# When the queries and keys of two pairs of heads are scaled: behind their roots, or in front of their turns

## The chip, the core and the metric

The kernel runs on one core of a Trainium2 chip. The metric is the device time of one execution in microseconds (us). The engines have a queue each and run it in order: TensorE (PE, matrix products; PEld is its weight load), VectorE (DVE), ScalarE (ACT), GpSimd (POOL) and SyncE (SP), which here only issues transfers. An instruction that waits for another engine holds everything behind it on its own queue.

## The reference

There are 8 batch elements of 12 heads, 448 positions and 64 channels a head. The first half is attention with normalised queries and keys, the second an MLP mixer over positions and then over channels. Cut to what matters:

```python
q_n = q / sqrt(mean(q*q, -1) + 1e-6) * g_q          # the same for k
attn = softmax(q_n @ k_n.T / 8)                      # per head, 448 x 448
x = (attn @ v) laid out as (8, 448, 768)
h = relu(x^T @ w_tok1) @ w_tok2                      # over positions: 448 -> 256 -> 448
u = x + h^T
out = u + relu(u @ w_ch1) @ w_ch2                    # over channels: 768 -> 1536 -> 768
```

The weights of the mixer come in 64-bit floats and are converted to 32 bits by the kernel.

## The kernel before

**Work.** The heads go in pairs, 6 pairs to an element, 48 in all, and two pairs at a time (`t`) make an attention step of four parts (`s` = 0 to 3, written `g = 4t + s`). The attention of an element runs beside the mixer of the element before it: two lists of items with a cost each are merged in proportion (`merge`), and the merged list is written out in that order. The engines' queues follow it as written; only the order on SP's queue is chosen by the scheduler. `behind` holds what follows a part's score and value products (`tiled`) in the attention list, `turns` the transposes of the next two pairs.

**Normalising a pair `n`.** Its queries and keys are loaded to `qk_t` (L1371). ACT squares them (`square`, L1391), DVE sums the squares by row (`reduce`, L1408). For two pairs together `roots` forms the reciprocal roots: DVE makes a first guess (`guess`, L1430), then POOL refines it in three rounds of four small instructions (`newton`, L1438 to L1441). `scale` (L420, DVE) multiplies the pair's queries and keys by the roots in place. `turn_qk` then transposes them: for the first two elements ("plain" pairs, `n` under 12) by 16 PE transposes a two pairs (L432), four for each half of a pair, whose results ACT copies out (L438, L440).

**Around the change.** The pairs that it touches are 8 to 11, the last four of the second element. While they are prepared, the attention of pairs 6 to 9 runs beside the mixer of the first element:
- `score` (L458, PE) and its exponentials (L462, ACT); `group_sums` (L499, DVE) adds up exponentials for the softmax's denominators; `values` (L531, PE); the denominators' sums (L511, PE) and their reciprocals (L555 to L577, DVE).
- `tok2` (L879, PE) makes six products of two matmuls, each into one of two PSUM tiles `m_ps`; the addition L884 (DVE) adds a product to `uT` and frees its tile.
- `first_stage` (L969, PE) is the first element's channel mixer.
- `weight_items` converts a chunk of weights: transfers L222, five DVE instructions (L379 for the chunk three items earlier, then L345, L346, L348, L350), one on ACT (L356) and the store L234 or L237.
- POOL forms sums of weights (`some`, L249 to L266).

Of the kernel before, what the change touches and what calls it, by code (L numbers as in the profile page):

```python
# [83 lines left out]
def whole(ctx, tc, shifted, pre, q, k, v, g_q, g_k, moe_w_tok1, moe_w_tok2, moe_w_ch1, moe_w_ch2, out):  # L84
# [67 lines left out]
    st = dict(pre.st)  # L152
# [263 lines left out]
    def scale(p):  # L416

        x, d = pre.by_rows(p, st["qk", p])
        r = st.pop(("rs", p))
        nc.vector.tensor_tensor(out=x, in0=x, in1=r.unsqueeze(2).to_broadcast(list(x.shape)), op=ALU.mult)  # L420

    def turn_qk(p, i):

        qk = st["qk", p]
        if ("qkT", p) not in st:
            st["qkT", p] = pre.qkT[p] if p < len(pre.qkT) else qkT_pool.tile([P, 2, S], F32, name="qkT")[:]
        to = st["qkT", p][:, i, :]
        if pre.plain(p):
            ps = s_tile("t_ps")
            for c in range(NS):  # L430
                o = (i * NS + c) * P
                nc.tensor.transpose(ps[:, c * R:(c + 1) * R], qk[0:R, o:o + P], ident[0:R, 0:R])  # L432
            src = ps[:, 0:S]
        else:
            nc.vector.transpose(out=to, in_=qk[:, i * S:(i + 1) * S])
            src = to
        if i == 0:
            nc.scalar.mul(to, src, g_t[:, 0:1])  # L438
        elif pre.plain(p):
            nc.scalar.copy(out=to, in_=src)  # L440
        if i == 0:
            st.pop(("qk", p))
# [213 lines left out]
    def att_step(g):  # L656


        t, s = divmod(g, 4)
# [50 lines left out]
        n = p + 2  # L710
        ahead, behind, turns = [], [], []
        f = lambda fn, *pairs: [lambda i=i: fn(i, st) for i in pairs]
        scales = lambda n: [lambda i=i: scale(i) for i in (n, n + 1)]
        if g in (1, 5):
            ahead, behind = f(pre.square, g // 4 * 2 + 4), f(pre.reduce, g // 4 * 2 + 4)
        elif g in (2, 6):
            ahead, behind = f(pre.square, g // 4 * 2 + 5), f(pre.reduce, g // 4 * 2 + 5)
        elif g in (3, 7):
            behind = pre.roots(g // 4 * 2 + 4, st)
        elif g in (4, 8):  # L720
            behind = scales(g // 4 * 2 + 2)
        if live and n < NP:
            late = n < 2 * NPAIR + 2
            if t >= NPAIR // 2 and late:
                if s == 1:
                    ahead, behind = f(pre.square, n), f(pre.reduce, n) + f(pre.square, n + 1)
                elif s == 2:
                    behind = f(pre.reduce, n + 1) + pre.roots(n, st) + scales(n)
            elif t >= NPAIR // 2:
                a, b = f(pre.square, n) + f(pre.reduce, n), f(pre.square, n + 1) + f(pre.reduce, n + 1)  # L730
                behind = (a, b + pre.roots(n, st), scales(n), [])[s]
            now = {2: [] if pre.plain(n) else [n], 3: [n, n + 1] if pre.plain(n) else [n + 1]}.get(s, [])
            turns = [lambda q=q, i=i: turn_qk(q, i) for q in now for i in (1, 0)]
# [481 lines left out]

    mixing = set()
    att_items = lambda lo, hi: [it for g in range(lo, hi) for it in att_step(g)]

    run(merge(
        att_items(0, 8) + merge(att_items(8, AHEAD * per + 1), x_items(0, 0)), weight_items(0, BEFORE)))  # L1220
    left, (some, sums) = [], sum_items()
    for b in range(B):
# [24 lines left out]
        if b + AHEAD < B and (shifted or b < 2):  # L1247
            att = att_items(lo, lo + 10) + x_items(b + AHEAD, 0)
            if shifted:
                att += att_items(lo + 10, lo + per)  # L1250
            elif not b:
                step = att_step(lo + per - 1)
                att += att_items(lo + 10, lo + per - 1) + step[:5] + x_items(1, 1) + step[5:]
            else:
                run(att[:6])
                ahead, block, beside, between = big_step(BIG, False)
                att = att[6:] + att_items(lo + 10, lo + per - 1) + ahead + [block] + beside + between
        elif b + AHEAD < B:
            t = (b + AHEAD) * NPAIR // 2
            blocks = [big_step(t + i // 2, i % 2) for i in range(1, NPAIR + 1)]  # L1260
            blocks[4][3].extend(x_items(b + 1, 0))
            early = place(early, blocks, [near(early, at) for at in BLOCKS])
# [263 lines left out]
```

## Time and profile before

| | us |
|---|---|
| median of three runs | 1302.79 (1302.38 to 1304.1) |
| the profiled execution | 1300.44 |
| its span, first to last instruction | 1298.5 |
| PE busy | 1250.2 (96%) |
| DVE busy | 793.8 (61%) |
| ACT busy | 392.3 (30%) |
| POOL busy | 383.4 (30%) |
| L420 on `qk_t`, 112x1024: one instruction | 1.22 |

The page gives busy times of the engines, the chain of work that ended last, and groups of instructions by source line; the timeline gives single instructions in order, with the idle time of the engine before each and the engine that ended it. PE's rows count two for each 32-bit matmul, so a product of L879 is four rows, and four transposes are four rows. Times within the span count from its first instruction.

### The profile page before, as it was taken

To read this page: it belongs to the slowest core of one execution; us is meant where nothing else is said; L and a number is where in the kernel's file an instruction comes from. 1 tells how busy PE (TensorE), PEld (TensorE's weight loads), DVE (VectorE), ACT (ScalarE), POOL (GpSimd) and SP (SyncE) were. 2 spreads that over 40 slices of the span, in tenths; PEclk is the share of its full clock that TensorE was granted. 3 is DMA by queue.
4 is the path that set the end of the run, shared out by engine and by line. 5 is a ranking of instruction groups with operands and counts; after the bars stand their busy time and mean duration, and the time that the engine had idled before them with its cause. 6 is when DMAs were issued, how large, how long until landed. Compare 5 with 4: busy or idle time off the path is not lost.

```text
span 1298.5 us, 20006 instructions
## 1 busy us (share of the span) xinstructions
PE 1250.2 (96%) x7228; PEld 889.8 (69%) x7228; DVE 793.8 (61%) x1229; ACT 392.3 (30%) x781; POOL 383.4 (30%) x641
## 2 busy tenths in 40 slices
PE   5998999997899999999999999999999999999996
PEld 3444444455654577895787868785887868797996
DVE  6988769754655256765658366765558456554233
ACT  5663433222322043312343034311343033300210
POOL 1303440047887012231132222231122322131231
PEclk9999999998999999999999999999999999999998
DMA  9667585997899567685766867595866964386553
GB/s 207 174 183 180 155 226 146 216 258 208 248 275 217 121 148 172 152 229 117 173 167 144 218 141 175 140 224 116 188 156 149 232 140 136 117 200 156 180 174 79
DMA packets 492864, 228.37 MB, mean 176 GB/s; under 512 B 375508, under 2 KB 453332, under 8 KB 492756
## 3 DMA queue, kind: packets, MB, share of 16 engines
q1 hardware_dynamic: 476178, 213.10, 66.6%
q0 software_dynamic: 3584, 12.06, 3.0%
q10 hardware_dynamic: 12994, 1.84, 0.8%
q8 instruction: 59, 0.97, 0.3%
q14 instruction: 49, 0.40, 0.1%
HBM read 184.26 MB, written 42.66 MB: 175 GB/s over the span
## 4 chain that ended last, share of the span: by engine, by line
PE 84%; DVE 6%; DMA 3%; POOL 2%; issue 2%; ACT 1%; SPq 1%; ACTq 0%; DVEq 0%; POOLq 0%
PE m_ps L999 23%; PE m_ps L1065 21%; PE s_ps L458 9%; PE o_ps L531 9%; PE m_ps L879 5%; PE m_ps L969 5%; PE m_ps L1048 4%; PE t_ps L837 2%; PE m_ps L837 2%; DMA ws<-raw 1%; PE m_ps L511 1%; PE d_ps L511 1%; POOL raw L320 1%; PE t_ps L432 1%; DVE raw L348 1%
## 5 line engine op out<-in xcount | busy, mean ns | idle before, releaser
L1065 PE MATMUL m_ps<-hb,unit 128*128 128x224 f32 x1440 | 277.2, 354 | 0.0
L1065 PEld LDWEIGHTS m_ps<-hb,unit 128*128 128x128 f32 x1440 | 271.0, 190 | 8.8 <-issue 7.7
L999 PE MATMUL m_ps<-tu,unit 128*128 128x224 f32 x1008 | 201.6, 355 | 1.3 <-ACT r L1009 1.3
L999 PEld LDWEIGHTS m_ps<-tu,unit 128*128 128x128 f32 x1008 | 189.1, 190 | 15.0 <-issue 9.9
L462 ACT ACTIVATE e<-s_ps 128x448 f32<-128x448 f32 x294 | 138.3, 549 | 174.6 <-PE s_ps L458 166.2
L999 PE MATMUL m_ps<-uT,unit 128*128 128x224 f32 x756 | 153.6, 358 | 13.7 <-DVE hb L1005 11.5
L999 PEld LDWEIGHTS m_ps<-uT,unit 128*128 128x128 f32 x756 | 144.0, 192 | 21.6 <-DVE hb L1005 13.0
L458 PE MATMUL s_ps<-qkT 64*64 64x448 f32 x1260 | 144.6, 545 | 0.8 <-ACT x L819 0.8
L531 PE MATMUL o_ps<-e,v 64*64 64x448 f32 x1148 | 131.4, 538 | 0.3 <-ACT uT L568 0.2
L1005 DVE TENSOR_TENSOR hb<-m_ps,r 128x448 f32<-128x448 f32 x63 | 39.1, 621 | 120.5 <-POOL r L1005 68.9
L499 DVE TENSOR_TENSOR es<-es,e 128x896 f32<-128x896 f32 x90 | 103.2, 1146 | 14.4 <-ACT e L462 9.0
L1005 POOL TENSOR_TENSOR hb<-r,r 128x448 f32<-128x448 f32 x21 | 23.8, 1135 | 245.4 <-ACT r L1021 245.4
L458 PEld LDWEIGHTS s_ps<-qkT 64*64 64x64 f32 x1260 | 45.7, 132 | 69.6 <-issue 60.1
L531 PEld LDWEIGHTS o_ps<-e,v 64*64 64x64 f32 x1148 | 46.4, 133 | 63.1 <-issue 58.4
L1006 ACT ACTIVATE hb<-hb 128x448 f32<-128x448 f32 x84 | 48.4, 577 | 111.8 <-DVE hb L1005 76.6
L879 PE MATMUL m_ps<-w_sb,h 128*128 128x448 f32 x192 | 75.3, 544 | 3.3 <-DVE uT L884 3.3
L1438 POOL TENSOR_TENSOR nt<-rs 128x56 f32<-128x56 f32 (+1 forms) x57 | 19.5, 341 | 198.1 <-DVE rs L1430 195.1
L1080 POOL TENSOR_TENSOR uT<-uT,r 128x448 f32<-128x448 f32 x42 | 51.4, 1240 | 78.3 <-DVE r L1080 46.6
L320 POOL TENSOR_TENSOR raw<-raw 128x128 f32<-128x128 f32 x128 | 68.0, 551 | 16.1 <-DMA ws<-raw 5.9
L884 DVE TENSOR_TENSOR uT<-uT,m_ps 128x448 f32<-128x448 f32 x48 | 29.3, 613 | 63.0 <-PE m_ps L879 63.0
L1005 DVE TENSOR_TENSOR r<-m_ps,r 128x448 f32<-128x448 f32 x42 | 26.1, 622 | 64.7 <-PE m_ps L999 64.7
L1408 DVE TENSOR_REDUCE ms<-sq 128x28 f32<-128x896 f32 (+2 forms) x44 | 47.4, 1080 | 28.6 <-ACT sq L1394 25.0
(141 smaller groups left out, 1585.0 us busy)
## 6 DMA issues: line engine op xcount, KB each, us to landing
unit<-ws SPq DMA_DIRECT2D x267, 384.0 KB, 4.1
raw<-in_moe_w_ch_dram SPq DMA_DIRECT2D x72, 256.0 KB, 3.5
v<-in_v_dram SPq DMA_DIRECT2D x96, 112.0 KB, 3.9
xs<-xt SPq DMA_DIRECT2D x56, 168.0 KB, 4.4
out_dram<-turned SPq DMA_DIRECT2D x168, 56.0 KB, 2.0
qk_t<-in_q_dram SPq DMA_DIRECT2D x144, 56.0 KB, 3.7
qk_t<-in_k_dram SPq DMA_DIRECT2D x144, 56.0 KB, 3.6
x<-xs SPq DMA_DIRECT2D x42, 192.0 KB, 4.1
```

The lines of the kernel that those rows point to most:

```text
L320: nc.gpsimd.tensor_tensor(out=at[o], in0=at[x], in1=at[y], op=ALU.add if op == "+" else ALU.subtract)
L458: nc.tensor.matmul(out=pss[i][rows_of(i, a), 0:S], lhsT=qkT[h, 1, k * D:(k + 1) * D], rhs=qkT[h, 0, :], start=True, stop=True)
L462: nc.scalar.activation(out=e[:, i, :], in_=pss[i][:, 0:S], func=AF.Exp)
L499: nc.vector.tensor_tensor(out=es[:], in0=(es if k > 1 else st["e", t, 0])[:], in1=st["e", t, k][:], op=ALU.add)
L531: nc.tensor.matmul(out=st["o", p][a * D:(a + 1) * D, 0:S], lhsT=vt[rows, k * D:(k + 1) * D], rhs=e[rows, :], **kw)
L837: nc.tensor.matmul(out=st["t1", h][jc][:, 0:HC], lhsT=w1_sb[:, c, jc * P:(jc + 1) * P], rhs=st["x", b, h][:, :, c, :], start=start and c = ...
L879: nc.tensor.matmul(out=ps[:, 0:S], lhsT=st["h1", jc][:, cc * P:(cc + 1) * P], rhs=w2_sb[:, jc].rearrange("p c r -> p (c r)"), start=(jc == ...
L969: nc.tensor.matmul(out=ps, lhsT=a[:, o + 2 * half, :], rhs=natural(half * KF + t) if wide else u[:, half * KC + t, :], start=(t == 0 and h ...
L999: nc.tensor.matmul(out=ps[:, j * HS:(j + 1) * HS], lhsT=w[:, t, j, :], rhs=m, start=(t == 0), stop=(t == KC - 1))
L1005: add = lambda e, o, x, y: e.tensor_tensor(out=o, in0=x, in1=y, op=ALU.add)
L1048: nc.tensor.matmul(out=ps, lhsT=w[:, t, :], rhs=natural(half * KF + t), start=(half == 0 and t == 0), stop=(half == 1 and t == KF - 1))
L1065: nc.tensor.matmul(out=ps[:, x * HS:(x + 1) * HS], lhsT=st["w"][:, tile_at % 6, :], rhs=hb[:, X_SLOT[f], i, :], start=(i == 0), stop=(i == 3))
```

## The change

`scales(n)` leaves part 2 of the step, where it followed the roots, and joins part 3, where it stands ahead of `turns`. This concerns `n` = 8 and 10, that is pairs 8, 9 and 10, 11; `n` = 12 keeps its place.

```diff
                 if s == 1:
                     ahead, behind = f(pre.square, n), f(pre.reduce, n) + f(pre.square, n + 1)
                 elif s == 2:
-                    behind = f(pre.reduce, n + 1) + pre.roots(n, st) + scales(n)
+                    behind = f(pre.reduce, n + 1) + pre.roots(n, st) + ([] if pre.plain(n) else scales(n))
+                elif s == 3 and pre.plain(n):
+                    behind = scales(n)
```

No instruction is added or removed. Since two items of 0.4 each go from one side of the part's products to the other, the merge also sets other items differently. In the queues of the two programs as built, a conversion standing for its five instructions:

```
PE, first place
  before: L879 p1, L879 p2, L458 + L531, L879 p3, 4 x L432, L879 p4, 12 x L432, L879 p5, ...
  after:  L879 p1, L458 + L531, L879 p2, L879 p3, 4 x L432, L879 p4, 12 x L432, L879 p5, ...
DVE, first place (pairs 8, 9)
  before: L1430, L420, L884, L420, conversion A, L884 x2, L499, conversion B, L499, L884 x2, ...
  after:  L1430, L884, conversion A, L884 x2, L499 x2, conversion B, L420 x2, L884 x2, ...
DVE, second place (pairs 10, 11)
  before: L1430, conversion, L420 x2, conversion, L499 x2, conversion, ...
  after:  L1430, conversion, L499, conversion, L499, L420 x2, conversion, ...
SP, first place
  before: key loads of pair 10, query loads, then loads and stores of weights between them
  after:  two weight loads and a weight store stand ahead of those key loads
```

ACT's and POOL's queues are the same in both.

## The prediction

> **What bounds the kernel now.** I read the page first: its chain of waits says that the end is set by TensorE (PE).
>
> ```profile
> PE 84%; DVE 6%; DMA 3%; POOL 2%; issue 2%; ACT 1%; SPq 1%; ACTq 0%; DVEq 0%; POOLq 0%
> ```
>
> A microsecond that PE loses is therefore lost for good, unless a later wait on the same chain has another cause. The moved instructions (L420) lie at 106 to 109 us and 147.6 to 150 us. For PE between 80 and 300 us the view of waits shows how often it stood still, with total, number and longest:
>
> ```profile
> PE m_ps L879 <- DVE uT L884: 3.3, 2, 2.8
> ```
>
> Both of these waits lie at the first place. The timeline of VectorE (DVE) there (start, length, instruction, idle time before it) shows why:
>
> ```profile
> 101.96 0.18 DVE L1430 TENSOR_SCALAR rs<-ms 112x32 int32<-112x32 int32 x1
> 106.06 1.23 DVE L420 TENSOR_TENSOR qk_t<-qk_t,rs 112x1024 f32<-112x1024 f32 x1 [3.92 <-POOL rs L1441]
> 107.20 0.61 DVE L884 TENSOR_TENSOR uT<-uT,m_ps 128x448 f32<-128x448 f32 x1
> 107.73 1.22 DVE L420 TENSOR_TENSOR qk_t<-qk_t,rs 112x1024 f32<-112x1024 f32 x1
> 108.87 0.69 DVE L379 SCALAR_TENSOR_TENSOR stages<-raw 128x512 f32<-128x512 f32 x1
> ...
> 112.13 1.14 DVE L884 TENSOR_TENSOR uT<-uT,m_ps 128x448 f32<-128x448 f32 x2
> 113.19 1.08 DVE L499 TENSOR_TENSOR es<-es,e 128x896 f32<-128x896 f32 x1
> 114.19 0.68 DVE L379 SCALAR_TENSOR_TENSOR stages<-raw 128x512 f32<-128x512 f32 x1
> ...
> 117.22 1.34 DVE L499 TENSOR_TENSOR es<-es,e 128x896 f32<-128x896 f32 x1
> ```
>
> DVE stands 3.92 us behind GpSimd's (POOL) roots, with the additions L884 queued behind the scaling. They free the two PSUM tiles of the token products (L879), so PE stands as well:
>
> ```profile
> 101.02 3.17 PE L879 MATMUL m_ps<-w_sb,h 128*128 128x448 f32 x8
> 104.12 1.74 PE L458 MATMUL s_ps<-qkT 64*64 64x448 f32 x16
> 105.67 1.68 PE L531 MATMUL o_ps<-e,v 64*64 64x448 f32 x16
> 107.87 1.77 PE L879 MATMUL m_ps<-w_sb,h 128*128 128x448 f32 x4 [0.52 <-DVE uT L884]
> 109.48 0.55 PE L432 MATMUL t_ps<-ident,qk_t 112*128 112x112 f32 x4
> 112.79 1.77 PE L879 MATMUL m_ps<-w_sb,h 128*128 128x448 f32 x4 [2.76 <-DVE uT L884]
> 114.40 1.31 PE L432 MATMUL t_ps<-ident,qk_t 112*128 112x112 f32 x12
> 115.55 1.68 PE L879 MATMUL m_ps<-w_sb,h 128*128 128x448 f32 x4
> ```
>
> I call the products p1 to p6, and a conversion the five DVE instructions L379 to L350. From 112.79 on PE runs without a gap to 193 us; the chain goes on through ScalarE's exponentials to DVE, which is busy until 249.7 us. All of that follows PE's time at 112.79.
>
> **First place: what goes.** DVE's wait of 3.92 us for the roots, and with it PE's 0.52 and 2.76 us for L884. That is 3.28 us on the path, if nothing takes their place.
>
> **First place: what comes instead.** In the new order the attention block (L458, L531) stands ahead of p2, and on DVE the two scalings stand behind L884 #1, conversion A, L884 #2 and #3, both sums L499 and conversion B. PE's order keeps the first four transposes (one half of the first pair) behind p3. The walk, by start-to-start times of the rows above:
> - PE: p1 101.02; block 102.57 (a product takes 1.55); p2 105.74 (the block takes 3.17, as from 149.06 to 152.23); p3 107.29; at 108.90 PE wants the transposes.
> - DVE: L884 #1 can start 1.70 after p1's start (as 268.22 to 269.92), at 102.72, and takes 0.53. Conversion A ends at about 106.3. #2 waits for p2 until 107.44, #3 for p3 until 108.99; that one ends at 109.52.
> - Behind #3 come two sums. 2.2 us is what a pair took at 130.13; one beside POOL work took 1.34 instead of 1.08, so 2.7 at most: 111.7 to 112.2. Then conversion B: 2.86 alone (86.78 to 89.64), 3.26 beside POOL (108.87 to 112.13): 114.6 to 115.5. Then one scaling, 1.23: 115.8 to 116.7. POOL's sums fall into this time, so I take the middle, 116.25.
> - PE starts the four transposes at 116.3 (0.38, a third of the 1.15 for twelve), p4 at 116.7 (1.61), twelve transposes at 118.3 (1.15), p5 at 119.4.
>
> p5 started at 115.55 before. So PE is 3.85 us later (3.4 to 4.3), although both old waits are gone: a wait of about 7.3 us at the transposes takes their place, and behind it on PE's queue stand p4 to p6, the next attention steps and the whole first channel stage. DVE itself gains about 1.2 us (these instructions ended at 118.48, now near 117.3), which helps nobody, as it then waits for p4 and p5.
>
> **The clock.** A wait that long has a second price. The trace has one other PE wait of this kind, 9.06 us ahead of 315.39. The windows of one microsecond around it (columns: stretch, length, busy time of PE, PEld, DVE, ACT, POOL, then the granted clock, DMA share, GB/s):
>
> ```profile
> 308.00:309.00 1.00, 0.00 (x0) 0.00 (x0) 0.00 (x0) 0.00 (x0) 0.92 (x3) 1.00 0.00 0
> 309.00:310.00 1.00, 0.00 (x0) 0.00 (x0) 0.00 (x0) 0.00 (x0) 0.92 (x4) 0.86 0.00 0
> 310.00:311.00 1.00, 0.00 (x0) 0.00 (x0) 0.00 (x0) 0.00 (x0) 0.94 (x3) 0.50 0.00 0
> 319.00:320.00 1.00, 1.00 (x4) 0.92 (x3) 0.81 (x2) 0.00 (x0) 0.84 (x3) 0.52 1.02 352
> 320.00:321.00 1.00, 1.00 (x7) 0.99 (x6) 0.00 (x0) 0.53 (x1) 0.92 (x3) 1.00 0.79 170
> ```
>
> PE went idle at 306.33, the clock halved near 309.7, 3.4 us later, and was whole again near 320.0, 4.6 us after PE had started again. Half of 4.6 us is lost: 2.3 us. The old wait of 2.76 us kept a clock of 1.00. The new one of 7.3 us lies on the side of the long one, so I add 2.3. The ends: 0, if it counts like the short one; (4.6 + 3.4) / 2 = 4.0, if the return comes one such interval later.
>
> [...]
>
> **Second place.** DVE waits 2.39 us ahead of L420 at 147.64, but PE has no gap there, so removing it buys nothing. The new order is sum, conversion, sum, two scalings. The first sum needs the exponentials that begin at 150.13 (two take 0.98), so 151.1; 1.1 later the conversion, 2.9 to 3.3; a sum, 1.1; the scalings end at 157.4 to 157.8 and 158.6 to 159.0. The transposes start at 158.34, and those of the second pair after eight of them, at 159.1. Cover: 0.1 to 0.5 us for the second scaling. I price it at nothing. Without the cover it costs what is late, at most some 1 us if both sums run beside POOL. The conversion behind it ends 2.9 later than before, but the next one stood 2.06 us behind ScalarE, and L560 at 166.27 stood 2.40 us behind PE, so that dies out.
>
> **Queues.** ScalarE's and POOL's orders do not change. The first roots now run beside conversion A: 3.8 us alone (102.22 to 106.03), 5.2 beside a conversion (142.43 to 147.60), so they end by 107.4, long before 114.6. On SyncE's queue two weight loads and a store pass ahead of the key load of the next pair, which waits for the four transposes. Its query loads were issued at 116.88 and now follow the transposes at 118.7; the squaring that waited for them (123.08) moves by less than PE does. Nothing there adds to the sum.
>
> **Sum.** 3.85 + 2.3 + 0 = 6.1 us on the chain. The profiled execution took 1300.44 us, 1298.5 of it span and 1.94 around it; it would take 1306.6. The median of the runs is 2.35 above that execution, so I forecast 1302.79 + 6.1 = 1308.9 us. This case alone reaches from +3.4 to +9.3.
>
> **Rivals.**
> - Faster: the scalings end before PE asks for them. Then only the old 3.28 us go: 1299.5 us. It decides at 108.9 us, the end of p3; my walk has the first scaling end 7.3 us after that. For it: DVE's wait of 3.92 us does go. Against it: DVE's order, for no duration in these rows varies by as much. Chance 0.08.
> - The clock stays whole: +3.85, 1306.6 us. For it: one long wait is all that the trace shows. Chance 0.20.
> - The delay dies out: PE's later wait of 9.06 us comes from POOL and from transfers, and would swallow it if these did not start later too: 1302.8 us. Against it: the chain leads from that POOL work back through SyncE's queue and DVE at 279 us to L879 at 277 us, that is to PE. Chance 0.12, from no change to +2.6.
> - The second place is late too, by 1 to 3 us: 1310 to 1312 us. Chance 0.05.
> - The forecast has 0.55.
>
> **From cases to numbers.** About 0.2% (2.6 us) is what a measurement of this kernel can tell from no change. Slower than that: 0.55 + 0.20 + 0.05 = 0.80; within it 0.12; faster 0.08. The range 1303.4 to 1312.0 takes in the forecast with nearly all its bounds, the whole clock, and the upper part of the delay that partly dies out; it leaves out the faster case and the delay that is gone.
>
> **What would show it.** Right: PE's first four transposes wait for DVE's L420 near 109 us for about 7 us, the waits of L879 for L884 are gone, L420 no longer waits for POOL, the granted clock shows 0.5 for some 4 to 6 us from about 115 us on, and the stage that began at 121.94 (L969) begins about 6 us later. Wrong: the transposes wait less than 3 us, or DVE reaches the scalings before conversion B; then the faster case holds. A clock of 1.00 from 110 to 125 us would leave 3.85. If L969 is late by 6 us and the end is not, the delay died out, and PE's wait at 306 us must be shorter by as much.

## The result, and the profile after

| | us |
|---|---|
| before, median of nine runs | 1303.03 (1301.95 to 1304.88) |
| after, median of nine runs | 1307.88 (1306.96 to 1313.45) |
| ratio after to before | 1.0041, 95% interval 1.0029 to 1.0054 |
| the profiled execution after | 1307.47, span 1305.7 |

The change makes the kernel slower by some 5.3 us (0.41% of 1303; the interval is 3.8 to 7.0). Two more lines in the source shift the line numbers: L881 is L879 of before, L886 is L884, L971 is L969, L1001 is L999, L1432 is L1430.

TensorE's timeline at the first place (start, length, instruction, idle time before it and what ended it):

```profile
100.43 1.67 PE L881 MATMUL m_ps<-w_sb,h 128*128 128x448 f32 x4
102.02 1.73 PE L458 MATMUL s_ps<-qkT 64*64 64x448 f32 x16
103.58 1.68 PE L531 MATMUL o_ps<-e,v 64*64 64x448 f32 x16
105.19 3.27 PE L881 MATMUL m_ps<-w_sb,h 128*128 128x448 f32 x8
116.48 0.98 PE L432 MATMUL t_ps<-ident,qk_t 112*128 112x112 f32 x4 [8.01 <-issue]
117.25 3.22 PE L881 MATMUL m_ps<-w_sb,h 128*128 128x448 f32 x4
120.26 1.81 PE L432 MATMUL t_ps<-ident,qk_t 112*128 112x112 f32 x12
121.91 1.68 PE L881 MATMUL m_ps<-w_sb,h 128*128 128x448 f32 x4
```

The waits of the products for VectorE's additions are gone, and 8.01 us stand ahead of the first four transposes instead. The profile calls what ended them "issue"; VectorE's timeline, with GpSimd's behind it, shows what stood in the way:

```profile
109.04 2.28 DVE L499 TENSOR_TENSOR es<-es,e 128x896 f32<-128x896 f32 x2
111.24 0.95 DVE L379 SCALAR_TENSOR_TENSOR stages<-raw 128x512 f32<-128x512 f32 x1
112.11 0.67 DVE L345 TENSOR_SCALAR cv_sb<-raw 128x512 uint32<-128x512 uint32 x1
112.82 0.82 DVE L346 SCALAR_TENSOR_TENSOR raw<-raw,cv_sb 128x512 f32<-128x512 uint32 x1
113.68 0.82 DVE L348 SCALAR_TENSOR_TENSOR raw<-raw 128x512 uint32<-128x512 uint32 x1
114.54 0.71 DVE L350 TENSOR_SCALAR raw<-raw 128x512 uint32<-128x512 uint32 x1
115.17 2.34 DVE L420 TENSOR_TENSOR qk_t<-qk_t,rs 112x1024 f32<-112x1024 f32 x2
```

```profile
110.47 1.17 POOL L249 TENSOR_TENSOR few<-few 128x128 f32<-128x128 f32 x1 [1.78 <-DMA few<-ws]
111.60 0.90 POOL L250 TENSOR_TENSOR few<-few 128x128 f32<-128x128 f32 x1
112.46 0.63 POOL L251 TENSOR_TENSOR few<-few 128x128 f32<-128x128 f32 x1
113.17 0.78 POOL L252 TENSOR_TENSOR few<-few 128x128 f32<-128x128 f32 x1
114.25 0.77 POOL L256 DMA_DIRECT2D ws<-few  x1 [0.29 <-POOL few L252]
```

The two sums and conversion B run first; the first of the two scalings takes 1.2 us from 115.17, and the transposes start at 116.48. No wait for the roots is left ahead of L420.

Then four transposes and p4 take 3.78 us (116.48 to 120.26) where they took 2.0 by the rows of before. The reason stands in the granted clock, the third column from the right in the windows of one microsecond:

```profile
110.00:111.00 1.00, 0.00 (x0) 0.00 (x0) 0.90 (x2) 0.00 (x0) 0.53 (x1) 1.00 0.42 156
111.00:112.00 1.00, 0.00 (x0) 0.00 (x0) 1.00 (x2) 0.00 (x0) 1.00 (x2) 0.52 0.02 8
120.00:121.00 1.00, 1.00 (x5) 0.73 (x4) 0.49 (x1) 0.00 (x0) 0.80 (x2) 0.50 0.73 234
121.00:122.00 1.00, 1.00 (x11) 1.00 (x10) 0.13 (x1) 0.74 (x2) 0.00 (x0) 0.86 0.00 0
122.00:123.00 1.00, 1.00 (x4) 0.50 (x4) 0.00 (x0) 1.00 (x3) 0.00 (x0) 1.00 0.61 140
```

The clock is halved from 111.0 to about 121.3 us (a mean of 0.86 in the stretch from 121 to 122 puts its return there), so 4.8 us of TensorE's work after the restart ran at half speed.

From p1's start to p5's start it is now 21.48 us against 14.53 before. This distance, which I call the first place's length, moves by less than a tenth of a microsecond from one execution to the next (14.53 and 14.60 in two profiles of the kernel before) and is the finer measure in what follows.

### The profile page after: what moved, and what is told of

It is laid out like the page before. It is cut to its first block, busy times and chain, and to the rows that moved or that the text cites. A ratio compares the mean times of both kernels' runs of the same rounds, so it can differ in the third digit from the quotient of the medians.

```text
span 1305.7 us, 19999 instructions
## 1 busy us (share of the span) xinstructions
PE 1252.8 (96%) x7228; PEld 890.2 (68%) x7228; DVE 795.1 (61%) x1229; ACT 391.8 (30%) x781; POOL 384.9 (29%) x641
## 4 chain that ended last, share of the span: by engine, by line
PE 84%; DVE 5%; DMA 4%; issue 2%; POOL 2%; SPq 1%; ACT 1%; DVEq 0%; POOLq 0%; ACTq 0%
PE m_ps L1001 23%; PE m_ps L1067 21%; PE s_ps L458 9%; PE o_ps L531 8%; PE m_ps L881 6%; PE m_ps L971 5%; PE m_ps L1050 4%; PE m_ps L839 3%; PE t_ps L839 2%; DMA ws<-raw 1%; PE d_ps L511 1%; POOL raw L320 1%; PE m_ps L511 1%; DMA v<-in_v_dram 1%; DVE raw L346 1%
## 5 line engine op out<-in xcount | busy, mean ns | idle before, releaser
L1001 PE MATMUL m_ps<-tu,unit 128*128 128x224 f32 x1008 | 201.6, 355 | 1.3 <-ACT r L1011 1.3
L1001 PEld LDWEIGHTS m_ps<-tu,unit 128*128 128x128 f32 x1008 | 189.1, 190 | 15.0 <-issue 9.9
L1001 PE MATMUL m_ps<-uT,unit 128*128 128x224 f32 x756 | 154.3, 359 | 13.5 <-DVE hb L1007 12.1
L1001 PEld LDWEIGHTS m_ps<-uT,unit 128*128 128x128 f32 x756 | 144.6, 193 | 21.7 <-DVE hb L1007 13.6
L881 PE MATMUL m_ps<-w_sb,h 128*128 128x448 f32 x192 | 76.8, 553 | 0.3 <-DVE uT L886 0.3
L886 DVE TENSOR_TENSOR uT<-uT,m_ps 128x448 f32<-128x448 f32 x48 | 29.4, 614 | 76.4 <-PE m_ps L881 76.4
```

Source lines behind the costliest of these rows:

```text
L881: nc.tensor.matmul(out=ps[:, 0:S], lhsT=st["h1", jc][:, cc * P:(cc + 1) * P], rhs=w2_sb[:, jc].rearrange("p c r -> p (c r)"), start=(jc == ...
L1001: nc.tensor.matmul(out=ps[:, j * HS:(j + 1) * HS], lhsT=w[:, t, j, :], rhs=m, start=(t == 0), stop=(t == KC - 1))
```

## The experiments

The theory: TensorE's transposes wait for whatever stands on VectorE ahead of the scaling, the sums and conversion B above all, and that wait costs a second time by the clock. Its rivals: both places lose (A), the lower clock costs nothing (B), the new order of products and attention block costs by itself (C), what is gained or lost at this place dies out later (D), or something later gains as well (E). The diffs of first_only, second_only, filled and filled_more are against the changed kernel, the others against the kernel before and show the main lines alone. All but second_only move the scalings of pairs 8 and 9 alone. Line numbers shift again: L885 and L436 in filled_more are L879 and L432 of before, L884, L889 and L1446 in split are its L879, L884 and L1441.

**One place at a time.** `n` is 8 for pairs 8 and 9, 10 for pairs 10 and 11.

```diff
 # first_only
-                    ... + ([] if pre.plain(n) else scales(n))
-                elif s == 3 and pre.plain(n):
+                    ... + ([] if n == 8 else scales(n))
+                elif s == 3 and n == 8:
 # second_only: the same with n == 10
```

> Only the scaling of pairs 8 and 9 moves; pairs 10 and 11 stay as before. Theory (DVE's queue ahead of the scaling holds up PE's transposes, then the clock halves): the whole loss is here, +4.3 to +5.3 us against before, PE's wait at the first four transposes again about 8.0 us, granted clock 0.5 from about 111 to 121 us. Rival A (both places lose): about half of it, +2 to +3 us.

> Only the scaling of pairs 10 and 11 moves. Theory: PE has no gap there and loses at most the 0.4 us that the profile after shows at the second eight transposes; the total is within 1 us of before. Rival A: +2 to +3 us. DVE's wait for POOL's roots (2.39 us) goes and brings nothing.

Measured: first_only 1.0052 (1.0035 to 1.0069), with a wait of 8.01 us at the transposes, the clock halved from 112.7 to 123.0 us, and a first place of 21.90 us; its 6.8 us are more than the 4.3 to 5.3 expected, though the interval reaches down to 4.6. second_only 1.0010 (0.9998 to 1.0021), first place 14.54. first_only alone loses no less than the whole change, so rival A falls: the loss is the first place's. The second place is not quite free: from the eight rows of L971 ahead of the transposes to those behind them it is 5.16 us in second_only (155.10 to 160.26) and 5.13 after, against 4.54 before.

```profile
155.10 3.17 PE L971 MATMUL m_ps<-uT,stages 128*128 128x448 f32 x8
158.33 0.96 PE L432 MATMUL t_ps<-ident,qk_t 112*128 112x112 f32 x8
159.46 0.96 PE L432 MATMUL t_ps<-ident,qk_t 112*128 112x112 f32 x8 [0.18 <-ACT qkT L440]
160.26 3.19 PE L971 MATMUL m_ps<-uT,stages 128*128 128x448 f32 x8
```

The transposes run in two pieces, and the scalings of second_only, 2.35 us from 157.01, end at 159.36, just ahead of the second piece. The row names ScalarE's copy L440, which ended at 159.47; in before that copy ended at 159.52 and the sixteen transposes ran from 158.34 without a gap, so I put the 0.6 us down to the scalings. No run separates the two.

**Less in front of the scaling.** Two kernels take work away from between the products' additions and the first place's scalings, which leave part 2 as in first_only.

```diff
 # behind_sums: the scalings run inside the last sum's item, ahead of conversion B
 # (within = scales(n) for s == 3 and n == 8)
+            if within:
+                items[-1] = (0.5, lambda: [fn() for fn in [lambda: group_sums(t, 6)] + within])
+                behind = [lambda: None] * 2
 # before_sums: the scalings directly behind the part's products, ahead of both sums
         items.append((2.4 if s == 1 else 3.2, tiled))
+        items += part(early)          # early = scales(n) for s == 3 and n == 8
```

> As first_only, but the two scalings of pairs 8 and 9 stand directly behind the two sums L499, ahead of conversion B. Theory: the first scaling ends about 4 us earlier than in first_only (conversion B took 3.9), PE waits about 4.0 us in place of 8.0, and p5 starts about 15.2 us after p1 against 14.5 before and 21.5 after: +0.7 us against before with a whole clock, up to +2.7 if 4 us of idleness still halve it. Rival C (the order of the products and the attention block is what costs): as first_only.

> As first_only, but the two scalings of pairs 8 and 9 stand directly behind the products' additions L884 #2 and #3, ahead of both sums and conversion B. Theory: the first scaling ends 1.8 us after PE asks for it; p5 starts about 13.0 us after p1 against 14.5 before, the clock stays whole, and the kernel is 1.5 us faster than before. Rival C (the order of the products and the attention block costs by itself): slower than before by 3 us or more.

TensorE's first four transposes, in behind_sums and then in before_sums:

```profile
113.69 0.98 PE L432 MATMUL t_ps<-ident,qk_t 112*128 112x112 f32 x4 [4.35 <-issue]
110.56 0.57 PE L432 MATMUL t_ps<-ident,qk_t 112*128 112x112 f32 x4 [1.89 <-issue]
```

Measured: behind_sums 1.0019 (1.0006 to 1.0031). Its wait is 4.35 us, the clock is halved from 112.6 us to about 119.4, and the first place is 18.28 us long. A whole clock would have made 15.5 of it (12.39 to the transposes, and 0.38 + 1.61 + 1.15); the other 2.8 are the clock's, so here a wait of 4.35 us cost as much by the clock as one of 8.01 us (2.3 in the changed kernel, 2.7 in first_only). before_sums 0.9986 (0.9977 to 0.9995): the wait is 1.89 us, the clock stays at 1.00, the first place is 13.01 us, as expected, and the kernel beats the one before by a little. It has the order of products and attention block of the changed kernel, so rival C falls too.

**The merged order alone.**

```diff
 # merge_only: the scalings behind their roots as before, two empty items where the change puts them
+                    if n == 8:
+                        last = behind[-1]
+                        behind[-1] = lambda: [fn() for fn in [last] + scales(n)]
+                elif s == 3 and n == 8:
+                    behind = [lambda: None] * 2
```

> The scalings of pairs 8 and 9 stand directly behind their roots as before (both ahead of L884 #1), but two empty items of the same cost stand where the change puts them, so that the attention block stands ahead of p2 as in the changed kernel. Theory: the merged order by itself costs nothing; DVE waits for POOL again, p3 waits for L884 #1 and p4 for #2, and p5 starts about 14.2 us after p1 against 14.5 before: within 1 us of before. Rival C: most of the loss, +3 us or more.

Measured: 0.9989 (0.9978 to 1.0001), first place 14.56 us against 14.53. VectorE stands 3.89 us behind the roots again, and p3 and p4 wait 1.44 and 1.68 us. The order by itself is worth nothing that these runs can tell.

**The clock by itself.** Extra matmuls ahead of the first four transposes keep TensorE at work while it would wait; the transposes overwrite their result, and all else is first_only.

```diff
             ps = s_tile("t_ps")
+            for _ in range(8 if p == 8 and i == 1 else 0):     # filled_more: 10, and lhsT=w1_sb[:, 0, 0:P]
+                nc.tensor.matmul(
+                    out=ps[:, 0:S], lhsT=ident[:, :], rhs=w2_sb[:, 0].rearrange("p c r -> p (c r)"),
+                    start=True, stop=True)
```

> As first_only, with eight extra matmuls of 128x128 by 448 columns (6.2 us of PE work; their result is overwritten by the transposes) in PE's queue directly ahead of the first four transposes, so that PE works while it would wait. Theory: the transposes still start when the first scaling ends, about 16.0 us after p1 starts, so the wait's own 3.85 us or a little more stays, but the clock stays at 1.00 and its share of about 2.3 us goes: 1.8 to 2.9 us faster than first_only, about +2.5 us against before. Rival B (the lower clock costs nothing, since PE's work there is hidden behind DVE): same time as first_only.

> As filled, with ten extra matmuls (7.75 us) in place of eight, and weights w1_sb as their stationary operand in place of the identity, so that PE works until about 0.4 us before the first scaling ends. Theory: the granted clock stays at 1.00 through the restart; the four transposes start about 16.0 us after p1 and p5 about 19.2 us after it (21.9 in first_only, 20.8 in filled), which puts the clock's share at 2.7 us; the total is about +4.6 us against before. Rival B (the lower clock costs nothing): p5 again about 21.9 us after p1.

filled missed its aim. 1.96 us of waiting were left ahead of the transposes, and the clock halved all the same, from 117.4 to 120.8 us, behind the restart. The first place was 20.81 us, 1.1 less than in first_only where 1.8 to 2.9 less had been expected; the total, 1.0041 (1.0025 to 1.0056), is not told apart from first_only. filled_more left 0.46 us:

```profile
108.22 7.68 PE L431 MATMUL t_ps<-w_sb 128*128 128x448 f32 x20
116.36 0.60 PE L436 MATMUL t_ps<-ident,qk_t 112*128 112x112 f32 x4 [0.46 <-DVE qk_t L420]
116.80 1.68 PE L885 MATMUL m_ps<-w_sb,h 128*128 128x448 f32 x4
118.32 1.32 PE L436 MATMUL t_ps<-ident,qk_t 112*128 112x112 f32 x12
119.47 1.68 PE L885 MATMUL m_ps<-w_sb,h 128*128 128x448 f32 x4
```

Its windows show 1.00 throughout. The transposes start 16.01 us after p1, as in first_only (16.05), and here the profile names L420 as what they waited for; p5 starts 19.12 us after p1, against 21.90. So 2.8 us of first_only's loss at this place are the clock's, and rival B falls by the trace. The total, 1.0038 (1.0022 to 1.0054), is lower than first_only's by 1.8 us, but the two intervals overlap: the clock's share is shown in the trace, not in the totals.

**A better version, and the scatter.** Conversion A covers most of the time of the roots, so the first pair's scaling can stand right behind it.

```diff
 # split: pair 8's scaling at the end of the part's products, pair 9's behind the additions of p2 and p3
+                elif s == 3 and n == 8:
+                    within, early = scales(n)[:1], scales(n)[1:]
 ...
                 for k in ((), (0,), (1, 2), (3, 4))[s]:
                     values(pair, k)
+            for fn in within:
+                fn()
```

> As first_only, but the scaling of pair 8 stands between conversion A and L884 #2, and that of pair 9 behind #3: the roots have ended there (conversion A covers them) and nothing else is ahead. Theory: PE's transposes wait less than 0.5 us, both old waits of L879 for L884 are gone, p5 starts about 11.3 to 11.8 us after p1 against 14.5 before, and the kernel is 2.7 to 3.3 us faster than before, which is the faster case of the prediction. Rival D (a gain at this place dies out at a later wait): same time as before.

> The kernel split once more. Theory: -3.5 us against before, as p5's distance from p1 fell by 3.5 us (11.0 against 14.5); the -5.6 us of the first comparison holds some 2 us of scatter. Rival E (something later gains as well): -5 us or more again.

> The kernel before, unchanged, timed against itself, to see what a comparison of this size can tell and how far single profiled executions lie apart. All theories: ratio 1.000 within 0.15%, p5 14.5 us after p1, the span within 3 us of 1298.5.

Measured: split 0.9957 (0.9941 to 0.9972) and, in the second comparison, 0.9971 (0.9956 to 0.9986); the first place is 10.99 us in both, 3.54 less than before and 0.3 less than the least expected. VectorE's timeline of split:

```profile
103.66 0.72 DVE L379 SCALAR_TENSOR_TENSOR stages<-raw 128x512 f32<-128x512 f32 x1
...
107.84 1.23 DVE L420 TENSOR_TENSOR qk_t<-qk_t,rs 112x1024 f32<-112x1024 f32 x1 [1.10 <-POOL rs L1446]
108.98 1.15 DVE L889 TENSOR_TENSOR uT<-uT,m_ps 128x448 f32<-128x448 f32 x2
110.04 1.22 DVE L420 TENSOR_TENSOR qk_t<-qk_t,rs 112x1024 f32<-112x1024 f32 x1
```

and TensorE's:

```profile
109.30 0.55 PE L432 MATMUL t_ps<-ident,qk_t 112*128 112x112 f32 x4
...
116.95 0.98 PE L511 MATMUL d_ps<-es,one_c 64*64 64x448 f32 x8 [0.45 <-DVE es L499]
...
121.31 4.78 PE L974 MATMUL m_ps<-uT,stage 128*128 128x448 f32 x12 [0.17 <-DVE uT L889]
```

The scaling still waits 1.10 us for the roots, but nobody waits for it: the transposes of split start at 109.30 without a gap. This is the prediction's faster case, reached by another order on VectorE, and it beats both kernels. Part of what p5 gains is lost again right behind it, more than half of that in waits for VectorE that before does not have (0.45 and 0.17 us above): from p1 to the last products of the first channel stage it is 146.27 us (247.69) against 148.65 in before (249.67), so 2.4 of the 3.54 us are left there. So rival D holds for about a third of the gain, and falls for the rest. Rival E stays open: 2.4 us lie within the interval of the second comparison with before, not within that of the first. before_again came to 0.9997 (0.9982 to 1.0012) against itself; its span was 1301.0 us, 2.5 above that of the first profile.

The first place's length against the total, both as differences from before (the total from the ratio, at 1303 us):

| kernel | first place, us | total, us (interval) |
|---|---|---|
| split | -3.5 | -5.6 (-7.7 to -3.6), again -3.8 (-5.7 to -1.8) |
| before_sums | -1.5 | -1.8 (-3.0 to -0.7) |
| merge_only | 0.0 | -1.4 (-2.9 to 0.1) |
| second_only | 0.0 | 1.3 (-0.3 to 2.7) |
| behind_sums | 3.8 | 2.5 (0.8 to 4.0) |
| filled_more | 4.6 | 5.0 (2.9 to 7.0) |
| filled | 6.3 | 5.3 (3.3 to 7.3) |
| after | 7.0 | 5.3 (3.8 to 7.0) |
| first_only | 7.4 | 6.8 (4.6 to 9.0) |

The two rise together, nearly one for one; the first comparison of split and the 1.4 us of merge_only show how far single totals stray. A good part of the scatter sits in one later wait near 315 us, TensorE's at L999 for VectorE's L1005, which follows SyncE's transfers and GpSimd's sums. It differs between two executions of the same program; here is before_again:

```profile
317.18 7.58 PE L999 MATMUL m_ps<-uT,unit 128*128 128x224 f32 x24 [10.86 <-DVE hb L1005]
```

It was 9.06 us in the first profile of the same kernel; split had 9.52 and 11.88 (at its L1004).

## Why the prediction was right, point by point

- **The path.** Right. In nine kernels the total follows TensorE's time at p5. The loss did not die out at the later wait: in the five kernels that lost 3.8 us or more at p5 it is 9.51 to 11.00 us long, in the seven other profiles 9.06 to 11.93. The gain of split did lose a third on its way, see above.
- **The wait at the transposes.** Right in place and cause, undersized: 8.01 us against about 7.3. The walk put the transposes 15.3 us after p1; they came after 16.05. The rest of the walk (0.38, 1.61 and 1.15 us to p5) held to 0.03 us in filled_more (3.11), so the place without the clock costs 16.05 + 3.14 - 14.53 = 4.7 us, not 3.85 (3.4 to 4.3). The term that failed is conversion B: 3.93 us (111.24 to 115.17), above both prices taken, 2.86 alone and 3.26 beside GpSimd; the two sums took 2.2 us, the lower end of their price. Conversion B took the same 3.93 or 3.94 us in first_only and filled. GpSimd's sums L249 to L252 ran beside it from 110.47 on and its transfer's issue from 114.25 on, and each of its five instructions took longer than alone (from start to start 0.87, 0.71, 0.86, 0.86 and 0.63 us, against 0.60, 0.45, 0.73, 0.73 and 0.35 from 86.78 on in before). That GpSimd slowed it is read from this overlap; no run takes GpSimd's work away.
- **The clock.** Right in kind and size: 21.48 - 16.05 - 3.14 = 2.3 us, the predicted 2.3. That it is 2.3 exactly is luck: the same wait of 8.01 us cost 2.7 in first_only by the same sum. The stretch of 0.5 was announced from about 115 us on for 4 to 6 us; it lasted from 111.0 to 121.3, of which only the 4.8 us behind the restart cost anything.
- **The second place.** Priced at nothing with 0.1 to 0.5 us of cover, it costs 0.6. After the change the first sum took 1.65 us (157.50) and the conversion 3.50 (159.08 to 162.58), GpSimd working beside both, so the cover was gone. The upper bound of 1 us held.
- **The sum.** 6.1 forecast, 5.3 (3.8 to 7.0) measured. The trace's own sum is 6.95 + 0.6 = 7.5 us, and the two profiled spans differ by 7.2; but that span of before was a quick one, as before_again's 1301.0 shows. So the terms were 1.4 us too small, and the total came out lower than they are by 0.5 to 3.7 us. What takes this back is not settled: the later wait alone scatters by 2.9 us over the twelve profiles. That the forecast came within 1 us of the measured median is therefore in part luck.
- **The rivals.** That the clock stays whole (1306.6) was wrong at this place; the total alone could not have told, as +3.85 lies just within its interval. The faster case failed for the reason given, VectorE's order; split shows that another order on VectorE brings it about.

## What to carry to other kernels

An instruction taken out of a wait and put in front of its user inherits everything that is queued there: list what the engine runs between the last input and the moved instruction, and compare that sum with the moment when the user is ready. The best place tried here is behind work that nearly covers the wait, not as late as possible: the two scalings of the first place, put behind conversion A and behind the next additions instead of behind conversion B, turned a loss of 6.8 us (first_only) into a gain of 4 to 6. And a wait of TensorE is to be priced twice where it may halve the clock: the waits of 8.01 and 4.35 us cost another 2.3 to 2.8 us here, while those of 2.76 us in before and 1.89 us in before_sums left the clock at 1.00.

## What the runs showed of the hardware that was not expected

The clock fell 2.6 us after TensorE went idle in the changed kernel (108.5 to 111.0 us), 3.3 us after it in behind_sums (109.3 to 112.6), and 3.4 us in first_only (109.3 to 112.7) and at the later wait of before (306.3 to 309.7), while a wait of 2.76 and one of 2.84 us, in the two profiles of before, left it at 1.00. So in these runs no fixed length of wait decides. In filled a wait of 1.96 us, behind 6.2 us of matmuls with the identity as weights, was enough, while the 1.89 us of before_sums were not. Two rows of filled:

```profile
117.00:118.00 1.00, 1.00 (x6) 0.59 (x6) 0.92 (x1) 0.52 (x1) 0.00 (x0) 0.71 0.29 99
120.00:121.00 1.00, 1.00 (x7) 0.85 (x6) 0.60 (x1) 0.00 (x0) 0.86 (x2) 0.59 0.60 210
```

The low stretch there was 3.4 us long (117.4 to 120.8). filled_more changed the number of matmuls and the weights together, so whether the identity as weights plays a part is open.

The low stretches at these waits are multiples of one length. By the trace and by windows of 0.2 us the clock was at 0.50 for 3.41 us in filled, for 6.83 us in behind_sums (112.60 to 119.42), and for 10.24 us in the changed kernel (111.04 to 121.28 and again 319.25 to 329.49), in first_only (112.72 to 122.96) and at the later wait of before (309.72 to 319.96): one, two and three times 3.41. The two falls in the changed kernel lie 208.21 us apart, 61 times 3.413. In the last 3.41 us ahead of the fall TensorE had not worked at all in first_only, and for 0.15 us in behind_sums, 0.84 in the changed kernel and 1.46 in filled. That does not decide by itself: a stretch of this length around the whole wait holds 1.5 us of work in before_sums and 0.65 in before, and the clock stayed at 1.00. What decides is not shown; no run was made to test it.

Once TensorE worked again, the clock was whole after 4.0 us in filled, 4.6 at the later wait of before, 4.8 in the changed kernel, 5.6 in first_only and 5.7 in behind_sums. Half of the last three is 2.4, 2.8 and 2.9 us, close to their prices: 2.3 and 2.7 us for the same 8.01 us of waiting, 2.8 us for 4.35. So here the price of a wait followed the moment of the return and not the length of the wait.

Beside GpSimd's sums one conversion took 3.93 us in the changed kernel (111.24 to 115.17) against 2.86 alone in before (86.78 to 89.64), and GpSimd's L249 took 1.17 us at 110.47 against 0.47 at 119.07 in the profile of the changed kernel, where VectorE stood still: both were longer than alone. It is not always both. In behind_sums the conversion's L379 and L345 took 0.68 and 0.41 us (114.90 to 115.95), as alone (0.69 and 0.42 us at 86.78 in before), while the GpSimd instruction beside them ran for some 2.4 us by the windows of 0.2 us (about 113.9 to 116.3), longer than any of the four sums in the changed kernel.
